# Order of the sign DMAs and the loads of q and k, and the engine of X's low part for two pairs of heads

## The chip, the core and the metric

The kernel runs on one core of a Trainium2 chip. The metric is the device time of one execution in microseconds, the median of several executions. A core has TensorE (PE, the matmuls; PEld its weight loads), VectorE (DVE), ScalarE (ACT), GpSimd (POOL) and SyncE (SP), which here only issues DMAs. Each engine works through its own instructions in order and waits for others at semaphores. SP's DMAs run on the core's 16 DMA engines.

## What is computed

Attention with a mask of hashed buckets, followed by a mixture of experts with a fixed capacity.

```python
def attn(q, k, v, proj):                      # q, k, v: 4 x 8 x 768 x 64, proj: 64 x 6
    q_bits = (q @ proj > 0); k_bits = (k @ proj > 0)
    q_bucket = sum(q_bits * 2**arange(6)); k_bucket = sum(k_bits * 2**arange(6))
    scores = where(q_bucket == k_bucket, q @ k.T / 8, -1e9)
    scores -= scores.max(-1)
    a = exp(scores); a /= a.sum(-1) + 1e-9
    return a @ v
def moe(x, w_gate, w1, w2):                   # x: 3072 x 512, 8 experts of 384 tokens each
    # tokens are taken in falling order of their best gate logits, until an expert is full
    out[tokens of e] = relu(x[tokens of e] @ w1[e]) @ w2[e]
```

## The kernel before

The 32 heads are worked in 8 groups G of 4 (head h is j = h % 4 of group h // 4); the operands of two groups are held at a time, in buffers u = G % 2. float32 accuracy is made of pairs of 16-bit values, a high and a low part: `QA`, `KA` hold the high parts of q and k of a head with further rows below them, `QB`, `KB` the high part of one and the low part of the other. Rows 64 to 69 of `QA` and `KA` hold the six signs of the projections (in tile `bt` until they are moved), as large plus and minus values, so that one matmul gives scores that are far lower wherever a bucket differs. Rows 96 to 99 of `QA` take the row maxima.

Time goes in steps t, six per head (192 in all, and a few behind), each of two half-steps n = 2t and 2t + 1. Within a step each engine's program is written out by hand in the order `ORD` (line 23): `S` passes of a head some 9 to 12 steps ahead (`S_pass`, line 259: two matmuls into `pss`, line 267, and the row maximum by DVE, line 269), then the score matmuls of the step's head in two halves (`ST`, line 306: lines 316 and 317 into `pst`, one of three buffers, and the exponential by ACT, line 318), the low part of the exponentials (`lo`, lines 322 and 325, by POOL or DVE), the matmuls with v four steps later (`AV`, lines 339 to 341), and whatever lists of half-steps (`P1` to `P4`, `Z3`, `Z4`, `MV`, `MD`) put at n.

These lists prepare the next group. For group G + 1 q and k are loaded (`load`, line 75; `qp` and `kp` have one buffer each; the issuing line is 77), ACT casts q and k to their high parts `qh` and `kh` in four pieces each (`cast`, line 148; q's from half-step 48G + 22 on, k's from 48G + 29 on, 48 half-steps being one group), negates them into `ql` and `kl` (`turn`, line 152; from 48G + 28 on), POOL's DMA adds the float32 values to these (`adds`, line 154), PE projects and DVE takes the signs (lines 168 and 172). At the end `sumv` (line 231) sums v with twelve matmuls.

`moves` (line 193) then brings group G's parts into `QA`, `KA`, `QB` and `KB` by DMAs of SP, in up to four portions. For G = 3 to 6 the order is the string `MO` (line 47): `A`, `B`, `K`, `L` are the high parts, `c` clears the maxima's rows (line 216), `s` is eight DMAs of signs (line 206), two per head, `q` and `k` are the loads of the next group, `l` and `m` the low parts (`kb<-kl`, `qb<-ql`). The bars part the portions; the third and fourth stand at half-steps 105 and 111 for G = 3 and at 48(G-1) + 8 and + 15 for G > 3. Between them lie, on SP, the DMAs of the maxima (`m_lay`, line 287, `qa<-mr`), behind them the transposes and stores of the attention's result (`xout`, lines 377 and 378). `turn` writes the tile `ql` that the DMA `m` of the group before has read.

For each pair of heads, `xlow` (line 367) subtracts the high part of the normalised result X (`XS`, cast by ACT, line 365) from X. It is emitted 4 half-steps behind the cast, for odd heads h = 1 to 29, on POOL where `XE[0] <= h <= XE[1]`, else on DVE.

`S_pass` and `ST` call `holds`, which counts what `wrote` noted of a buffer when the program is built; it makes no instruction.

Of the kernel before, what the change touches and what calls it, by code (L numbers as in the profile page):

```python
# [24 lines left out]
 E0=[3, 5],  # L25
 E1=[],
 X=[5, 4, 20, 15],
 XE=[9,25],
 MR=3,
 MT=4,  # L30
 LEAD=[9,12,40,4],
# [12 lines left out]
 Z4=[-20,-12,-18,-9,-12,-6],  # L44
 EA=[262, 32, 5],
 EG={2: 0, 3: 3},
 MO=['', 'AKs', 'BqL', 'lmk', 'c|ABqKLslmk', 'AB|KL|cs|qklm', 'AB|KL|cs|qklm'],
 MD=[[0, 2], [0, 5, 9, 15], [0, 2, 7, 14]],
 MV=[23, 24, 28, 57, 96, 1],
 WS=-23,  # L50
# [6 lines left out]
def attention(tc, nc, ctx, qT, kT, vv, proj, wg, x_dram, L, jp, identf, ident, B, late=None, after=None):  # L57
# [10 lines left out]
    def wrote(w,G): KEEP[w,G%2]=KEEP.get((w,G%2),[])+[G]  # L68
    def holds(G,**need):
        for w,n in need.items():  # L70
            if KEEP.get((w,G%2),[])[-n:]!=[G]*n: raise ValueError(f'{w} of group {G} is read out of turn')
# [3 lines left out]
    def load(G,w):  # L75
        if w==0: alloc_load(G)
        SY.dma_start(LD[G][w],(qT,kT,vv)[w][G])
# [13 lines left out]
    def warm(n,w=512):  # L91
        for _ in range(n): T.matmul(wps[:,0:w],wrm[:,0:128],wrm[:,0:w],start=True,stop=True)
# [17 lines left out]
    QA=[];KA=[];QB=[];KB=[];VH=[];VL=[];WF=[]  # L110
# [32 lines left out]
    def cast(G,w,p,half=None):  # L143
        if (G,'h') not in TMP:
            TMP[G,'h']=[dp.tile([128,2,S],F16,name=n,bufs=1) for n in ("qh","kh")]
            TMP[G,'l']=[dp.tile([128,2,S],F16,name=n,bufs=1) for n in ("ql","kl")]
        if half is None: A.copy(TMP[G,'h'][w][:,p],LD[G][w][:,p])
        else: A.copy(TMP[G,'h'][w][:,p,half*384:half*384+384],LD[G][w][:,p,half*384:half*384+384])
    def sub(G,w,p,eng=None):
        (eng or G_).tensor_tensor(TMP[G,'l'][w][:,p],LD[G][w][:,p],TMP[G,'h'][w][:,p],op=ALU.subtract)  # L150
# [18 lines left out]
    def signs(G):  # L169
        bt=TMP[G,'b']=dp.tile([128,S],F16,name="bt",bufs=1); b2=bt.rearrange("p (z q) -> p z q",z=2); z=0  # L170
        for ps in TMP[G,'p']:
            n=ps.shape[1]; V.tensor_scalar(b2[:,z:z+n],ps[:,:,0:384],0.0,0.5,op0=ALU.is_gt,op1=ALU.subtract); z+=n
        if G in (2,3): scaled(G)
        elif G<2: V.tensor_scalar(bt,bt,8192.0,None,op0=ALU.mult)
# [4 lines left out]
    def his(G):  # L179
        u=G%2; h=TMP[G,'h']  # L180
        for qk,(a,b,r0) in enumerate(((QA,QB,0),(KA,KB,64))):
            for r,j in sides(G): SY.dma_start(a[u][0:64,j,0:S],h[qk][r,1])
            wrote('hi',G)
            for r,j in sides(G): SY.dma_start(b[u][r0:r0+64,j,:],h[qk][r,1])
    def dbits(G):
        u=G%2; bt=TMP[G,'b']
        for hh in range(2):
            for w,dst in enumerate((QA,KA)): SY.dma_start(dst[u][64:70,2+hh,0:S],bt[64+32*w+6*hh:70+32*w+6*hh,:])
        wrote('sign',G)
    def lows(G):  # L190
        u=G%2; l=TMP[G,'l']
        for r,j in sides(G): SY.dma_start(KB[u][0:64,j,:],l[1][r,1]); SY.dma_start(QB[u][64:128,j,:],l[0][r,1])
        wrote('low',G)
    def moves(G,part=0):


        u=G%2; h=TMP[G,'h']; l=TMP[G,'l']; bt=TMP[G,'b']
        hs=[(slice(64*hh,64*hh+64),slice(hh,4,2)) for hh in range(2)]
        def go(dst,src,r0=0):
            for r,js in hs: SY.dma_start(dst[u][r0:r0+64,js,0:S],src[r])  # L200
            wrote('hi' if dst is QA or dst is KA else 'low',G)
        def signs_():
            for j in range(4):
                for w,dst in enumerate((QA,KA)):
                    a=64*(j//2)+32*w+6*(j%2)
                    SY.dma_start(dst[u][64:70,j,0:S],bt[a:a+6,:])
            wrote('sign',G)
        def nxt(w):
            if G+1<NG: load(G+1,w)
        todo=dict(A=(go,QA,h[0]),B=(go,QB,h[0]),K=(go,KA,h[1]),L=(go,KB,h[1],64),s=(signs_,),c=(clear,G),q=(nxt,0),k=(nxt,1),l=(go,KB,l[1]),m=(go,QB,l[0],64))  # L210
        for x in AP['MO'][part] if G==1 else AP['MO'][min(G+2,6)].split('|')[part]:
            f,*x=todo[x]; f(*x)
    def clear(G):
# [3 lines left out]
    def cv(G,j):  # L217
        A.copy(VH[G%2][:,j,:,0:64],LD[G][2][:,j]); wrote(f'vh{j}',G)
    def sv(G,j,e=None,n=1):
        for i in range(j,j+n): holds(G,**{f'vh{i}':1}); wrote(f'vl{i}',G)  # L220
        (e or V).tensor_tensor(VL[G%2][:,j:j+n],LD[G][2][:,j:j+n],VH[G%2][:,j:j+n,:,0:64],op=ALU.subtract)
# [36 lines left out]
    M6={}; passes={}; maxed=[]  # L258
    def S_pass(h,qc):
        G,j=divmod(h,4); u=G%2  # L260
        if G: holds(G,hi=2,sign=1)
        if G>1: holds(G,clear=1)
        passes[h]=passes.get(h,0)+1
        if qc==0: M6[h]=m8[h%3]
        ps=psS.tile([128,2,512],F32,name="pss")
        for hf in range(2):
            T.matmul(ps[:,hf,0:HK],QA[u][:,j,qc*128:qc*128+128],KA[u][:,j,hf*HK:hf*HK+HK],start=True,stop=True)  # L267
            if h==0: warm(DW[1],DW[4])
        V.tensor_reduce(M6[h][:,qc:qc+1],ps[:,:,0:HK],axis=AX.XY,op=ALU.max,negate=True)  # L269
# [19 lines left out]
    def m_rows(h,hf):  # L289
        G,j=divmod(h,4)  # L290
        if passes[h]<(6 if h>=2 else 3*hf+3): raise ValueError('a maximum is not whole')
        maxed.extend([(h,0),(h,1)] if h>=2 else [(h,hf)])
        if h>=2:
            ps=psS.tile([128,2,512],F32,name="pss")
            for c in range(6):
                T.matmul(ps[:,c//3,c%3*128:c%3*128+128],M6[h][:,c:c+1].to_broadcast([128,128]),ident,start=True,stop=True)
            A.activation(QA[G%2][96:128,j,:].rearrange("p (z q) -> p z q",z=2),ps[96:128,:,0:384],AF.Relu,bias=mbi[96:128],scale=msc[96:128])
            return
        MR[hf]=psT.tile([128,512],F32,name="pst")
        for c in range(3):  # L300
            T.matmul(MR[hf][:,c*128:c*128+128],M6[h][:,3*hf+c:3*hf+c+1].to_broadcast([128,128]),ident,start=True,stop=True)
        A.activation(QA[G%2][96:128,j,hf*384:hf*384+384],MR[hf][96:128,0:384],AF.Relu,bias=mbi[96:128],scale=msc[96:128])
# [3 lines left out]
    def ST(h,kc,hf):  # L306
        G,j=divmod(h,4); u=G%2
        if (h,hf) not in maxed or h>=8 and h not in laid: raise ValueError('a head has no maximum')
        if G: holds(G,hi=2,sign=1)
        if G: holds(G,low=4)  # L310
        if hf==0 and kc%2==0:
            pl=PT[h,-1-kc]=(dp.tile([128,2,S],F32,name="pt",bufs=4),dp.tile([128,2,S],F16,name="lo",bufs=4))
            for i in range(2): PT[h,kc+i]=(pl[0][:,i],pl[1][:,i])
        ps=psT.tile([128,512],F32,name="pst")
        r=slice(hf*384,hf*384+384); kr=slice(kc*128,kc*128+128)
        T.matmul(ps[:,0:384],KA[u][:,j,kr],QA[u][:,j,r],start=True,stop=False)  # L316
        T.matmul(ps[:,0:384],KB[u][:,j,kr],QB[u][:,j,r],start=False,stop=True)  # L317
        A.activation(PT[h,kc][0][:,r],ps[:,0:384],AF.Exp,scale=0.125)  # L318
# [83 lines left out]
    def add(n,f,*a):  # L402
        if n>=2*(6*NH+LAG+6): raise ValueError('an operation has no step')
        at.setdefault(n,[]).append((f,a))
    def bdma():
        for w,a in enumerate((QA,KA)): SY.dma_start(a[0][64:70,1,0:S],TMP[0,'b'][32*w:32*w+6])
    def copies(a):
        for j in (0,2): SY.dma_start(a[1][64:128,j:j+2,0:S],a[0][64:128,2:4,0:S])
    OPS=dict(i=lambda j: init(j,A.copy),t=top,b=lambda n: tbits(),k=behind,P=lambda n: project(0,[1]),r=lambda n: rest(n//3,n%3),l=lambda n: rlo(n//2,n%2),
        c=lambda w: cast(0,w,1),u=lambda w: sub(0,w,1),s=lambda k: S_pass(k//6,k%6),B=lambda n: signs(0),D=lambda n: bdma(),  # L410
        m=lambda n: m_rows(n//2,n%2),d=lambda n: dbits(0),f=lambda n: lows(0),g=lambda n: his(0),v=lambda j: cv(0,j),x=lambda j: sv(0,j,G_),
        e=lambda k: ST(0,k,0),C=lambda n: copies((QA,KA)[n]),w=lambda n: warm(n,DW[4]))
    n=-1; early=[]
    for o in AP['OPS'].split():
# [30 lines left out]
    k=12; done={}; S_at={}  # L445
# [7 lines left out]
    for h in range(1,NH,2):  # L453
# [7 lines left out]
        else:  # L461
            add(n,xhigh,4*b+d); add(n+AP['X'][1],xlow,4*b+d,G_ if AP['XE'][0]<=h<=AP['XE'][1] else V)
        if h==NH-1: pass
# [586 lines left out]
```

## Time and profile before

| | us |
|---|---|
| median of 3 runs | 703.2 (701.91 to 705.95) |
| the profiled execution | 703.8 |
| its span, first to last instruction | 701.9 |
| mean granted TensorE clock | 0.974 |
| PE busy | 654.6 (93%) |
| DVE busy | 515.6 (73%) |
| POOL busy | 518.3 (74%) |
| ACT busy | 393.3 (56%) |

The attention fills about the first 376 us, the experts the rest. A time in a row is counted from the first instruction. PE's matmuls are pipelined and their ends are modelled, so the start-to-start distance of two is shorter than the time of one. SP's instructions have a start and the time that SP was taken up by them; when their data landed is seen where another engine's wait for them ends. The granted clock is 1.00 at 2.4 GHz and 0.50 at 1.2 GHz.

### The profile page before, as it was taken

To read this page: it belongs to the slowest core of one execution; us is meant where nothing else is said; L and a number is where in the kernel's file an instruction comes from. 1 tells how busy PE (TensorE), PEld (TensorE's weight loads), DVE (VectorE), ACT (ScalarE), POOL (GpSimd) and SP (SyncE) were. 2 spreads that over 40 slices of the span, in tenths; PEclk is the share of its full clock that TensorE was granted. 3 is DMA by queue.
4 is the path that set the end of the run, shared out by engine and by line. 5 is a ranking of instruction groups with operands and counts; after the bars stand their busy time and mean duration, and the time that the engine had idled before them with its cause. 6 is when DMAs were issued, how large, how long until landed. Compare 5 with 4: busy or idle time off the path is not lost. (4 is left out here: it accounts for less than half of the span.)

```text
span 701.9 us, 19028 instructions
## 1 busy us (share of the span) xinstructions
PE 654.6 (93%) x7761; PEld 420.4 (60%) x7769; DVE 515.6 (73%) x1217; ACT 393.3 (56%) x805; POOL 518.3 (74%) x473
## 2 busy tenths in 40 slices
PE   8999999999898999999996699999999999999994
PEld 2566676767576776677675565545455555545551
DVE  7879798878777778698887849898979797913110
ACT  6877786777766777675571253526171716253620
POOL 7799987979689597988740553859787878787751
PEclk9999999999999999999997599999999999999998
DMA  8639579767898589862121534353534434363501
GB/s 222 178 112 233 152 186 171 177 124 146 213 164 166 123 150 226 135 147 47 26 57 36 159 129 165 136 195 136 193 138 169 161 139 178 120 225 135 196 31 45
DMA packets 64299, 102.54 MB, mean 146 GB/s; under 512 B 28960, under 2 KB 53588, under 8 KB 62164
## 3 DMA queue, kind: packets, MB, share of 16 engines
q1 hardware_dynamic: 55880, 51.24, 31.3%
q0 software_dynamic: 8224, 50.08, 23.9%
q8 instruction: 61, 1.00, 0.6%
q14 instruction: 26, 0.21, 0.1%
q10 hardware_dynamic: 108, 0.01, 0.0%
HBM read 67.39 MB, written 12.58 MB: 114 GB/s over the span
## 5 line engine op out<-in xcount | busy, mean ns | idle before, releaser
L322 POOL TENSOR_TENSOR lo<-pt 128x768 f16<-128x768 f32 x148 | 244.9, 1756 | 47.7 <-ACT pt L318 44.7
L318 ACT ACTIVATE pt<-pst 128x384 f32<-128x384 f32 x384 | 174.5, 493 | 77.0 <-PE pst L317 73.2
L269 DVE TENSOR_REDUCE m<-pss 128x1 f16<-128x770 f32 x192 | 181.4, 956 | 37.3 <-PE pss L267 36.5
L316 PE MATMUL pst<-qa,ka 128*128 128x384 f16 x384 | 124.7, 325 | 7.4 <-ACT pt L318 6.2
L341 PE MATMUL psv<-vh,lo 128*128 128x65 f16 x1152 | 124.4, 194 | 0.7 <-POOL lo L322 0.5
L317 PE MATMUL pst<-qb,kb 128*128 128x384 f16 x384 | 124.8, 325 | 0.0
L339 PE MATMUL psv<-vh,pt 128*128 128x65 f16 x1152 | 124.6, 195 | 0.2 <-DVE X L357 0.2
L340 PE MATMUL psv<-vl,pt 128*128 128x64 f16 x1152 | 124.6, 193 | 0.0
L339 PEld LDWEIGHTS <-pt 128*128 128x128 bf16 x1152 | 107.4, 98 | 15.4 <-issue 3.1
L340 PEld LDWEIGHTS <-pt 128*128 128x128 bf16 x1152 | 106.1, 99 | 11.2
L867 ACT CAST wh<-wf 128x1024 f16<-128x1024 f32 x64 | 65.4, 1042 | 79.0 <-DMA wf<-in_w_dram,zwidx 50.0
L341 PEld LDWEIGHTS <-lo 128*128 128x128 f16 x1152 | 106.2, 98 | 1.1 <-POOL lo L322 0.8
L267 PE MATMUL pss<-ka,qa 128*128 128x385 f16 x384 | 94.2, 328 | 5.1 <-DVE m L269 4.3
L879 POOL TENSOR_TENSOR wl<-wf,wh 128x512 bf16<-128x512 f32 x74 | 84.2, 1153 | 0.0
L902 PEld LDWEIGHTS <-wh 128*128 128x128 f16 x544 | 50.6, 99 | 30.6 <-issue 0.9
L858 POOL DMA_INDIRECT wf<-in_w_dram,zwidx x20 | 20.5, 1024 | 57.2 <-DVE zmi L791 30.6
L914 PEld LDWEIGHTS <-hh 128*128 128x128 f16 x384 | 35.5, 98 | 36.2
L902 PE MATMUL ph<-xx,wh 128*128 128x384 f16 (+1 forms) x304 | 56.9, 312 | 0.1
L317 PEld LDWEIGHTS <-kb 128*128 128x128 f16 x384 | 37.2, 97 | 31.8 <-issue 10.7
L316 PEld LDWEIGHTS <-ka 128*128 128x128 f16 x384 | 37.6, 98 | 25.2 <-issue 2.6
L902 PE MATMUL po<-xx,wh 128*128 128x384 f16 x240 | 48.1, 326 | 0.0
L989 POOL TENSOR_TENSOR wl<-wf,wh 128x512 bf16<-128x512 f32 x36 | 42.7, 1212 | 5.5 <-ACT wh L867 5.3
(293 smaller groups left out, 1222.1 us busy)
## 6 DMA issues: line engine op xcount, KB each, us to landing
vp<-in_vv_dram SPq DMA_DIRECT2D x8, 768.0 KB
x_dram<-XS SPq DMA_DIRECT2D x16, 384.0 KB
qp<-in_qT_dram SPq DMA_DIRECT2D x7, 768.0 KB
kp<-in_kT_dram SPq DMA_DIRECT2D x7, 768.0 KB
qa<-qh SPq DMA_DIRECT2D x14, 192.0 KB
ka<-kh SPq DMA_DIRECT2D x14, 192.0 KB
qb<-qh SPq DMA_DIRECT2D x14, 192.0 KB
kb<-kh SPq DMA_DIRECT2D x14, 192.0 KB
```

Of the source, the lines that this page charges most:

```text
L267: T.matmul(ps[:,hf,0:HK],QA[u][:,j,qc*128:qc*128+128],KA[u][:,j,hf*HK:hf*HK+HK],start=True,stop=True)
L269: V.tensor_reduce(M6[h][:,qc:qc+1],ps[:,:,0:HK],axis=AX.XY,op=ALU.max,negate=True)
L316: T.matmul(ps[:,0:384],KA[u][:,j,kr],QA[u][:,j,r],start=True,stop=False)
L317: T.matmul(ps[:,0:384],KB[u][:,j,kr],QB[u][:,j,r],start=False,stop=True)
L318: A.activation(PT[h,kc][0][:,r],ps[:,0:384],AF.Exp,scale=0.125)
L322: eng.tensor_tensor(l,p,p.bitcast(BF)[:,1::2],op=ALU.subtract)
L339: T.matmul(av[:,c,:],ph[:,r],VH[u][:,j,kc,:],start=(kc==0 and c==0),stop=False,skip_group_check=True)
L340: T.matmul(av[:,c,0:64],ph[:,r],VL[u][:,j,kc,:],start=False,stop=False,skip_group_check=True)
L341: T.matmul(av[:,c,:],l[:,r],VH[u][:,j,kc,:],start=False,stop=False,skip_group_check=True)
L867: s.nc.scalar.copy(h[:,r],f[:,r])
L879: for _ in range(n): s.nc.gpsimd.tensor_tensor(*s.pend.pop(0)[1],op=ALU.subtract)
L902: T.matmul(p[:,r],a[:,o:o+128],b[:,d,r],start=n==0 and not c,stop=n==11 and c in (None,2),skip_group_check=c is not None)
```

## The change

Three edits. In `MO`, for the groups 3 and above, the third portion was clear, all signs, and the fourth the loads of q and k and the low parts; now the third is clear, the signs of heads j = 0 and 1 (`e`), and the load of q, and the fourth is the load of k, the signs of heads j = 2 and 3 (`o`), and the low parts. `signs_` takes the heads as arguments, and `holds` asks for two notes of signs for j > 1. `XE` ends at 21 in place of 25, so `xlow` of the pairs that end in heads 23 and 25 is DVE's.

```diff
- XE=[9,25],
+ XE=[9,21],
...
- MO=['', 'AKs', 'BqL', 'lmk', 'c|ABqKLslmk', 'AB|KL|cs|qklm', 'AB|KL|cs|qklm'],
+ MO=['', 'AKs', 'BqL', 'lmk', 'c|ABqKLslmk', 'AB|KL|ceq|kolm', 'AB|KL|ceq|kolm'],
...
-        def signs_():
-            for j in range(4):
+        def signs_(*js):
+            for j in js:
                 for w,dst in enumerate((QA,KA)):
                     a=64*(j//2)+32*w+6*(j%2)
                     SY.dma_start(dst[u][64:70,j,0:S],bt[a:a+6,:])
             wrote('sign',G)
...
-        todo=dict(...,s=(signs_,),c=(clear,G),q=(nxt,0),k=(nxt,1),...)
+        todo=dict(...,s=(signs_,0,1,2,3),e=(signs_,0,1),o=(signs_,2,3),c=(clear,G),q=(nxt,0),k=(nxt,1),...)
...
-        if G: holds(G,hi=2,sign=1)
+        if G: holds(G,hi=2,sign=1+(G>2 and j>1))
```

## Rows read from the trace of the kernel before

**Rows 1.** Busy table of the page: busy us, share, instructions.
```profile
PE 654.6 (93%) x7761; PEld 420.4 (60%) x7769; DVE 515.6 (73%) x1217; ACT 393.3 (56%) x805; POOL 518.3 (74%) x473
```
**Rows 2.** PE's waits, 115 to 290 us: who <- for whom: us, times, longest.
```profile
PE pst L316 <- ACT pt L318: 6.0, 14, 1.1
PE pst L282 <- ACT pt L318: 1.2, 4, 0.3
```
**Rows 3.** ACT's waits, 115 to 290 us.
```profile
ACT qh L148 <- DMA qp<-in_qT_dram: 7.0, 4, 2.4
...
ACT ql L152 <- DMA qb<-ql: 3.2, 3, 1.1
```
**Rows 4.** Timeline of ACT: start, us, engine, line, operation, [idle before <- releaser].
```profile
177.45 0.51 ACT L148 CAST qh<-qp 128x384 f16<-128x384 f32 x1 [2.21 <-DMA qp<-in_qT_dram]
...
184.64 0.84 ACT L152 ACTIVATE ql<-qh 128x768 f16<-128x768 f16 x1 [1.00 <-DMA qb<-ql]
...
222.46 0.51 ACT L148 CAST qh<-qp 128x384 f16<-128x384 f32 x1 [2.38 <-DMA qp<-in_qT_dram]
```
**Rows 5.** Timeline of SP in the moves of group 4, from the fifth sign on.
```profile
168.29 0.66 SPq L206 DMA_DIRECT2D qa<-bt  x1
169.93 0.66 SPq L206 DMA_DIRECT2D ka<-bt  x1
...
172.43 0.68 SPq L287 DMA_DIRECT2D qa<-mr  x1
173.15 0.44 SPq L77 DMA_DIRECT2D qp<-in_qT_dram  x1
173.65 0.42 SPq L77 DMA_DIRECT2D kp<-in_kT_dram  x1
...
175.63 1.43 SPq L200 DMA_DIRECT2D qb<-ql  x2
```
**Rows 6.** Stretches: PE, PEld, DVE, ACT, POOL busy, granted clock, DMA share, GB/s.
```profile
172.00:174.00 2.00, 2.00 (x29) 1.42 (x27) 1.93 (x6) 1.76 (x5) 2.00 (x3) 1.00 0.11 25
176.00:178.00 2.00, 1.44 (x24) 0.94 (x23) 2.00 (x4) 0.55 (x2) 2.00 (x3) 1.00 1.07 332
182.00:184.00 2.00, 2.00 (x40) 1.54 (x36) 1.46 (x2) 1.26 (x3) 1.76 (x3) 1.00 1.41 154
```
**Rows 7.** Timeline of SP, moves of group 5: fifth sign and load of q.
```profile
212.43 0.66 SPq L206 DMA_DIRECT2D qa<-bt  x1
...
216.14 0.55 SPq L77 DMA_DIRECT2D qp<-in_qT_dram  x1
```
**Rows 8.** Timeline of ACT: the maxima that the DMA at 172.43 moves.
```profile
168.80 0.44 ACT L284 ACTIVATE mr<-pst,mb,ms 24x128 f16<-24x128 f32 x1
```
**Rows 9.** A stretch as in rows 6; line 231's matmuls (ns min/median/max, first and last start).
```profile
226.00:228.00 2.00, 2.00 (x13) 1.40 (x12) 0.00 (x0) 0.01 (x1) 2.00 (x2) 0.50 0.93 46
...
L231 PE MATMUL pst<-vl,on x6: 270/270/271, 180.5 to 181.6; 128*128 128x256 f16 x6
...
L231 PE MATMUL pst<-vl,on x6: 416/417/418, 225.5 to 227.6; 128*128 128x256 f16 x6
```
**Rows 10.** Timeline of POOL: X's low part of head 23; low parts around 331.
```profile
305.40 1.65 POOL L367 TENSOR_TENSOR XS<-X,XS 128x768 f16<-128x768 f32 x1
...
331.04 5.03 POOL L322 TENSOR_TENSOR lo<-pt 128x768 f16<-128x768 f32 x3 [0.48 <-ACT pt L318]
```
**Rows 11.** Timeline of DVE: a maximum near head 23's step; two subtractions of one size.
```profile
304.76 0.96 DVE L269 TENSOR_REDUCE m<-pss 128x1 f16<-128x770 f32 x1 [0.62 <-PE pss L267]
...
331.51 1.80 DVE L322 TENSOR_TENSOR lo<-pt 128x768 f16<-128x768 f32 x1
...
341.72 0.95 DVE L322 TENSOR_TENSOR lo<-pt 128x768 f16<-128x768 f32 x1
```
**Rows 12.** PE's waits, 296 to 345 us.
```profile
PE pss L267 <- DVE m L269: 0.8, 2, 0.4
PE pss L396 <- DVE m L269: 0.2, 1, 0.2
```

More of the change, by code (lines that the diff above doesn't have):

```diff
@@ L209, in nxt @@
             if G+1<NG: load(G+1,w)
-        todo=dict(A=(go,QA,h[0]),B=(go,QB,h[0]),K=(go,KA,h[1]),L=(go,KB,h[1],64),s=(signs_,),c=(clear,G),q=(nxt,0),k=(nxt,1),l=(go,KB,l[1]),m=(go,QB,l[0],64))
+        todo=dict(A=(go,QA,h[0]),B=(go,QB,h[0]),K=(go,KA,h[1]),L=(go,KB,h[1],64),s=(signs_,0,1,2,3),e=(signs_,0,1),o=(signs_,2,3),c=(clear,G),q=(nxt,0),k=(nxt,1),l=(go,KB,l[1]),m=(go,QB,l[0],64))
         for x in AP['MO'][part] if G==1 else AP['MO'][min(G+2,6)].split('|')[part]:
@@ L308, in ST @@
         if (h,hf) not in maxed or h>=8 and h not in laid: raise ValueError('a head has no maximum')
-        if G: holds(G,hi=2,sign=1)
+        if G: holds(G,hi=2,sign=1+(G>2 and j>1))
         if G: holds(G,low=4)
```

## The prediction

> **What bounds the kernel now.** I read the busy table first [rows 1]: TensorE is busy for 654.6 of 701.9 us, so the kernel gets faster only where TensorE stands still or runs slowly. In the steady part of the attention, 115 to 290 us, the waits of TensorE are nearly all for the exponentials of ScalarE [rows 2]: 6.0 us before the score matmuls and 1.2 us before the matmuls that turn the maxima. So the next view is what ScalarE itself waits for [rows 3]. Waits for TensorE are harmless there; two others are not: 7.0 us in four waits for the load of q, and 3.2 us in three waits for the DMA `qb<-ql`. ScalarE works in order, so the exponentials queued behind a waiting cast wait too, the score tiles fill up, and TensorE stops. The timeline shows both kinds [rows 4]: 2.21 us at 177.45 for q of group 5, 2.38 us at 222.46 for q of group 6, 1.00 us at 184.64 for `ql`. The four q waits belong to the loads of groups 4 to 7, one in each.
>
> Why q is late stands in the timeline of the DMA-issuing engine, SyncE [rows 5]: in group 4 the eight sign DMAs go out one after the other, about 0.70 us each; the maxima's row `mr` follows directly, at 172.43, and q only at 173.15. Meanwhile the DMA engines do next to nothing: 0.11 busy from 172 to 174, but 1.07 and 1.41 from 176 to 178 and 182 to 184 [rows 6]. The load stands behind small DMAs that are not urgent, with an idle stretch ahead of it.
>
> **The change part by part: order on SyncE, groups 3 to 6** (group 7 has no next load; its signs alone are split, which costs nothing, since the signs of heads 2 and 3 are read at least 24 half-steps later). It removes and adds no DMA. q moves ahead of four signs and of `mr`: it takes the place of the fifth sign, 168.29 instead of 173.15, 4.9 us earlier. In group 5's moves the same step is 212.43 against 216.14 [rows 7], 3.7 us earlier. Now q is in use 177.45 - 173.15 = 4.3 us after its issue in one, 222.46 - 216.14 = 6.3 us in the other. Taking those: in use at 172.6, wanted at 177.45 - 2.21 = 175.24; and at 218.7, wanted at 220.08. The smallest margin is 1.3 us, so the four q waits should go.
>
> Next is what else the queue does. `mr` is ready by 169.24 [rows 8], so it need not wait long. k follows `mr`. The sixth sign went out 0.98 us late although its tile was free; that looks like a limit on DMAs under way (the eighth DMA before it is the first `kb<-kh`), and I let `mr` and k meet that wait instead: `mr` about 169.9, k about 170.95 (now 173.65). Then the four late signs, 4 x 0.70 = 2.8 us, to about 174.2, then `kb<-kl` and `qb<-ql` at 174.2 and 175.7, where they are now (175.63 for the second pair). So the low parts are issued no earlier, but q (768 KB) and k have mostly passed by then.
>
> That matters: **the wait for `ql` decides whether the gain is kept.** If ScalarE loses its q wait it comes to the `ql` step 2.2 us earlier, at 183.64 - 2.21 = 181.4 in group 5; if `qb<-ql` still landed at 184.64 it would only wait there for 3.2 us. An estimate of when it lands after the change: the four low DMAs are 192 KB each; at the 200 GB/s or so between the 154 and 332 GB/s of [rows 6] that is 3.9 us; starting 1.4 us after the first issue (175.6), with 1 us to be seen, 180.5. That is 0.9 us before it is wanted.
>
> The sum, ScalarE waits against TensorE time. *q waits:* -7.0 us. Behind each, ScalarE has the exponentials that were held up to catch up on, and TensorE lives from these, so I take a wait that goes as time gained one for one; bounds 0 (given back at `ql`) and -7.0. *`ql` waits:* bounds 0 and -3.2; I take -2.0, because the casts of k and the sign turns that follow keep ScalarE fuller than TensorE and leave some of TensorE's wait in place. *Clock:* in the one group with the longest q wait the granted clock is 0.50 from 226 to 228, which is 1.2 GHz, after TensorE stood still at the q wait; six sum matmuls `pst<-vl` then start over 2.1 us, against 1.1 us in the group before [rows 9]. Without the halt I expect no fall: -1.0 us, bounds 0 and -1.8. The granted clock fell after only one of the four halts, so an uncovered halt elsewhere may cost as much.
>
> **X's low part of heads 23 and 25.** Each goes from GpSimd (1.65 us [rows 10]) to VectorE; 2 x 1.65 = 3.3 us leave GpSimd, which gains nothing, because TensorE's waits in this stretch are for VectorE's maxima, 0.8 and 0.2 us, and for no low part of GpSimd [rows 12]. VectorE takes a 128x768 subtraction in 0.95 us, or 1.80 us while GpSimd works beside it [rows 10, 11]. Head 23's falls near 305, where VectorE has one gap of 0.62 us [rows 11]; if the maxima behind it (`pss`) come late, TensorE waits for them. Cost of each: 0.95 - 0.62 = 0.3 us of lateness at best, 1.80 - 0.62 = 1.2 us at worst, part of which the two `pss` buffers absorb. I take +0.4 for both; bounds -0.3 (a shorter GpSimd queue) and +2.4.
>
> The Trainium skill (SBUF — State Buffer, Who interferes with whom) has a rule against this part: a VectorE operation with two SBUF inputs and a GpSimd operation that reads SBUF take the shared port in turn, and the later one blocks for the whole of the other. The trace agrees on the direction (0.95 against 1.80 us) but shows 0.85 us of it, not a whole operation of GpSimd; what a whole one would give is rival 5, 697.8 us.
>
> Sum: -7.0 - 2.0 - 1.0 + 0.4 = -9.6. The profiled execution took 703.8 us (span 701.9 and 1.9 around it), 0.6 above the median of 703.2. 703.8 - 9.6 = **694.2 us**.
>
> **The rivals.** *1. The wait moves to `ql`.* q is in time, but the low parts still land when they do now, for instance because each DMA lands about 8 us after its issue whatever is ahead (`qb<-ql` issued by 177.06, used at 184.64). For it: they are issued no earlier. Against it: the queue ahead of them is then q and k, 1.5 MB that go earlier. Then the gain is lost in the three groups with a `ql` wait and kept in group 6 alone, 2.4 + 1.0 - 0.4 = 3.0: 700.8 us. *2. Half comes back elsewhere:* TensorE moves up to other limits, VectorE's maxima or GpSimd's low parts, as both are busy over 70% of the span. -4.8: 699.0 us. *3. It does not do what it says:* q still goes out late, because SyncE is held before it by a buffer or by DMAs under way. Against it: nothing holds the fifth sign, and q's buffer is free, since the signs that are being sent were made from it. 703.8 + 0.4 = 704.2 us. *4. Slower: the four late signs push the low parts back.* Place: SyncE between k and `kb<-kl`. If `mr` or k go out no earlier than now, the 2.8 us of signs come on top, `qb<-ql` is issued 2.8 us later in each group, and ScalarE waits that much longer for `ql` in the three groups where it waits already: 3 x 2.8 = +8.4, 712.2 us. It decides from the point where `qb<-ql` lands later than at 184.64 in that stretch: each us beyond that costs up to 3. *5. X's low part waits for a whole operation of GpSimd,* 1.65 us [rows 10], before its own 0.95: 2.6 - 0.62 = 2.0 us of lateness for each, 4.0 in place of 0.4: 697.8 us. Against it: the subtraction beside GpSimd's took 1.80, not 2.6 [rows 11].
>
> **How the numbers follow.** Forecast 0.58 (its own range 691.5 to 697.5: all of the waits, the clock at 1.8 and X's part at -0.3 give 703.8 - 12.0 - 0.3 = 691.5; two thirds of the q waits and no gain of clock give 703.8 - 4.7 - 2.0 + 0.4 = 697.5); rival 2, 0.11; rival 5, 0.04; rival 1, 0.12; rival 3, 0.09; rival 4, 0.06. A measurement of this kernel can tell about 0.5%, 3.5 us, from no change. Faster by more than that: the forecast, rivals 2 and 5 and a third of rival 1's spread, 0.77; same: the rest of rival 1 and rival 3, 0.17; slower: 0.06. The range must leave out no more than 2 in 10, so it goes from 691.5 to 701.0, which takes in rivals 1, 2 and 5.
>
> **What would show it.** In the changed profile: q issued directly behind the fourth sign; no wait of a q cast for its load in groups 4 to 7; `qb<-ql` used before 181.4 on the old time scale, and the `ql` waits near 0; no fall of the granted clock at about 225 us; TensorE's wait for the exponentials from 115 to 290 us down from 6.0 to about 2 us; the attention's end some 9 us earlier and everything behind it only shifted. I am wrong if the q waits go and the `ql` waits grow by as much, if TensorE begins to wait for `pss` or low parts in their place, or if the q waits stay.

## The result and the profile after

The changed kernel takes 693.8 us (median of 6 executions, 691.99 to 698.64); the kernel before took 702.75 us beside it. The ratio is 0.988, 95% interval 0.984 to 0.992. In a second comparison, beside the last experiments, it was 692.64 against 706.22 us, ratio 0.984 (0.980 to 0.988). The kernel before was 3.5 us slower there, so across the two comparisons ratios are compared, not times. The profiled execution took 694.53 us, its span is 692.6.

The waits of ScalarE from 115 to 290 us come first, as in [rows 3] (who <- for whom: us, times, longest). The line of the q casts is gone, and of 3.2 us for `ql` 0.7 are left.

```profile
ACT pt L318 <- PE pst L317: 36.6, 55, 2.9
...
ACT ql L152 <- DMA qb<-ql: 0.7, 1, 0.7
```

TensorE's waits in the same stretch answer to [rows 2]: 6.0 us for the exponentials before the score matmuls became 2.4. A small new one, for VectorE's copy of the maxima (line 277), has come up in the place of the 1.2 us at line 282. The sums of v (line 231) waited as well; in the kernel before it was

```profile
PE pst L231 <- ACT pt L318: 1.2, 4, 0.3
```

and in the changed kernel:

```profile
PE pst L316 <- ACT pt L318: 2.4, 5, 0.9
PE pst L282 <- DVE m L277: 0.7, 3, 0.2
PE pst L231 <- ACT pt L318: 0.2, 1, 0.2
```

The timeline of SyncE in the moves of group 4, to be read beside [rows 5]: q directly behind the fourth sign, then the maxima, k, four signs, the low parts.

```profile
166.64 0.66 SPq L206 DMA_DIRECT2D ka<-bt  x1
167.34 0.44 SPq L77 DMA_DIRECT2D qp<-in_qT_dram  x1
168.65 0.69 SPq L287 DMA_DIRECT2D qa<-mr  x1
170.02 0.33 SPq L77 DMA_DIRECT2D kp<-in_kT_dram  x1
170.57 0.69 SPq L206 DMA_DIRECT2D qa<-bt  x1
...
173.48 1.38 SPq L200 DMA_DIRECT2D kb<-kl  x2
174.96 1.37 SPq L200 DMA_DIRECT2D qb<-ql  x2
```

ScalarE's timeline at the two steps of [rows 4]: neither has an idle time in front of it now.

```profile
174.03 0.50 ACT L148 CAST qh<-qp 128x384 f16<-128x384 f32 x1
...
180.46 0.83 ACT L152 ACTIVATE ql<-qh 128x768 f16<-128x768 f16 x1
```

The DMA engines, by stretches as in [rows 6]: the stretch in front of the q cast that was idle (0.11) is in use.

```profile
168.00:170.00 2.00, 2.00 (x37) 1.47 (x34) 0.96 (x1) 1.95 (x6) 2.00 (x2) 1.00 0.88 211
...
172.00:174.00 2.00, 2.00 (x35) 1.48 (x34) 2.00 (x2) 1.54 (x5) 2.00 (x4) 1.00 0.82 330
```

Where the time went is best read from two stretches that are cut at the first exponential of a head: heads 8 to 23, in which the moves of groups 3 to 6 lie, and heads 24 to 30, in which X's part lies. The columns are those of [rows 6]. The kernel before:

```profile
113.02:292.65 179.63, 170.50 (x2627) 122.06 (x2626) 138.44 (x194) 129.67 (x303) 146.44 (x122) 0.99 0.82 162
292.65:362.17 69.52, 68.04 (x1135) 51.27 (x1133) 58.69 (x85) 43.56 (x101) 57.03 (x38) 1.00 0.37 80
```

and the changed kernel:

```profile
113.70:283.39 169.69, 166.36 (x2627) 120.62 (x2626) 138.60 (x194) 129.91 (x303) 146.38 (x122) 1.00 0.81 172
283.39:351.96 68.57, 67.67 (x1135) 51.08 (x1134) 59.63 (x87) 43.40 (x100) 53.44 (x36) 1.00 0.38 81
```

So heads 8 to 23 are 9.94 us shorter and heads 24 to 30 0.95 us. Of the 9.94 us, 5.8 come out of TensorE's idle time (179.63 - 170.50 = 9.13 became 169.69 - 166.36 = 3.33); 4.1 come out of the time that the profile counts as busy, the fall of the clock of [rows 9] among them. So the waits that a view lists need not be all that the halts cost. What lies ahead of head 8 is 0.68 us longer (113.70 against 113.02), what lies behind the start of head 31 is 0.9 us longer (692.6 - 351.96 against 701.9 - 362.17). Neither is touched by the change. The sum is -9.3 us of span.

### The profile page after: what moved, and what is told of

It reads as the page before. It is cut to its first block, busy times and chain, and to the rows that moved or that the text cites. A ratio compares the mean times of both kernels' runs of the same rounds, so it can differ in the third digit from the quotient of the medians.

```text
span 692.6 us, 19032 instructions
## 1 busy us (share of the span) xinstructions
PE 649.3 (94%) x7769; PEld 419.3 (61%) x7769; DVE 517.2 (75%) x1219; ACT 393.6 (57%) x805; POOL 514.7 (74%) x471
```

## The experiments

The theory under test: ScalarE's waits for q and for `ql` held up the exponentials, TensorE lost about as much, and the new order takes both away; X's part is small. The table puts the two waits (summed over heads 8 to 23) beside the length of heads 8 to 23 and of heads 24 to 30 in each profiled execution, and the ratio of the times with its interval.

| kernel | waits for q, `ql` | heads 8 to 23 | heads 24 to 30 | ratio to before |
|---|---|---|---|---|
| before | 7.0 + 3.2 | 179.63 | 69.52 | 1 |
| changed | 0 + 0.7 | 169.69 | 68.57 | 0.988 (0.984 to 0.992) |
| changed, again | 0 + 0 | 169.42 | 68.59 | 0.984 (0.980 to 0.988) |
| order alone | 0 + 0 | 169.25 | 69.51 | 0.986 (0.982 to 0.990) |
| X's part alone | 7.5 + 3.7 | 178.58 | 68.58 | 1.002 (0.999 to 1.004) |
| low parts late | 0 + 6.3 | 175.76 | 68.58 | 0.998 (0.995 to 1.001) |
| q ahead of all signs | 0 + 5.7 | 174.53 | 68.59 | 0.992 (0.988 to 0.996) |
| q behind the maxima | 0 + 1.3 | 170.34 | 68.58 | 0.984 (0.980 to 0.988) |
| X's part of head 25 alone | 0 + 0.5 | 169.61 | 68.07 | 0.984 (0.980 to 0.988) |
| four signs last | 0 + 0 | 169.79 | 68.59 | 0.985 (0.982 to 0.988) |
| low parts, then q | 14.1 + 0 | 186.44 | 68.58 | one execution each: 710.54 against 707.83 us |

The granted clock fell in heads 8 to 23 once in the kernel before, once with the low parts late, once with q ahead of all signs, three times with the low parts ahead of q, and in none of the others.

**The new order alone.** The changed kernel with one line undone:

```diff
- XE=[9,21],
+ XE=[9,25],
```

> The new order of the sign DMAs and loads alone; X's low part of heads 23 and 25 stays on GpSimd. My theory (nearly the whole gain is ScalarE's waits for q and ql): no q wait in groups 4 to 7, the ql waits at 0.7 us or less, and a time of 694 to 696 us, that is 7.5 to 9 us below the kernel before. In heads 24 to 31 the trace of the changed kernel is about 1.0 us shorter than that of before, and I put that down to X's low part, so this kernel should lack it. Rival (X's part carries a good share, since it also frees GpSimd in the tail): 698 us or more.

Measured: 692.51 us, ratio 0.986; neither wait is left. The two stretches:

```profile
112.76:282.01 169.25, 166.24 (x2627) 120.70 (x2626) 138.64 (x194) 130.03 (x303) 146.41 (x122) 1.00 0.80 172
282.01:351.52 69.51, 68.03 (x1135) 51.25 (x1133) 58.67 (x85) 43.55 (x101) 56.98 (x38) 1.00 0.36 80
```

The order alone has the whole gain that the times show. The time is even 1.5 us below the lower end of what I expected, though heads 24 to 30 take 69.51 us as before.

**X's part alone.** The kernel before with `XE=[9,21]`:

```diff
- XE=[9,25],
+ XE=[9,21],
```

> X's low part of heads 23 and 25 on VectorE alone, order of DMAs as before. My theory: 701 to 703 us, about 1 us below the kernel before: a new wait of some 0.5 us of TensorE for VectorE in head 25, and head 28 about 1.4 us shorter, since VectorE's subtraction there no longer runs beside one of GpSimd (0.95 in place of 1.80 us). The four q waits stay, 7 us in all. My prediction's own figure for this part was +0.4 us, so 703 to 704. Rival (this part carries the gain): under 698 us.

Measured: 703.95 us, ratio 1.002 (0.999 to 1.004), no difference that can be seen. That is a miss of what I expected here (701 to 703 us) and lies where the prediction's own figure put it (703 to 704). The trace does show a difference:

```profile
115.08:293.66 178.58, 169.02 (x2627) 120.99 (x2626) 138.52 (x194) 129.52 (x302) 146.38 (x122) 1.00 0.81 163
293.66:362.24 68.58, 67.67 (x1135) 51.07 (x1134) 59.64 (x87) 43.40 (x100) 53.45 (x36) 1.00 0.40 81
```

Heads 24 to 30 take 68.58 us, as in each kernel with this part. The 0.94 us do not appear in the whole times, where what is ahead of head 8 and behind head 30 differs by as much and more from one execution to the next (head 8 starts 2.06 us later in this one than in the kernel before). The q waits are there as before (7.5 us). There is one more thing in this trace: the granted clock is 1.00 throughout heads 8 to 23, and though it waits a little longer than the kernel before, this stretch is 1.05 us shorter. I put that down to the one fall of the clock in the kernel before [rows 9].

**Low parts late.** The changed kernel with a fifth portion, 4 half-steps behind the fourth:

```diff
- 'AB|KL|ceq|kolm', 'AB|KL|ceq|kolm'
+ 'AB|KL|ceq|ko|lm', 'AB|KL|ceq|ko|lm'
- [0, 5, 9, 15], [0, 2, 7, 14]
+ [0, 5, 9, 15, 19], [0, 2, 7, 14, 18]
```

> The changed kernel with the low parts (kb<-kl, qb<-ql) of groups 3 to 7 in a portion of their own, 4 half-steps later, so that the transposes and stores of X go out before them; q is as early as in the changed kernel. Theory that the landing of qb<-ql decides whether the gain is kept: no q waits, but ql waits of 3 to 5 us in each of groups 4 to 7, and a time of 703 to 710 us, the gain given back or more. Rival (q's wait alone is the cost, and ScalarE has slack behind it): 693 to 697 us.

Measured: 701.74 us, ratio 0.998. q is in time everywhere, and the gain is given back, at the place that rival 1 named, though the waits are shorter (0.95 to 2.24 us in a group) and the time lower than I expected. The trace keeps more than the times do: heads 8 to 23 are 3.9 us shorter than in the kernel before, where the changed kernel has 9.94. A fall of the clock behind the first of its waits (1.98 us) is part of the loss. ScalarE's waits and the stretch:

```profile
ACT ql L152 <- DMA qb<-ql: 6.3, 4, 2.2
```

```profile
114.75:290.51 175.76, 168.73 (x2627) 121.56 (x2626) 138.72 (x194) 130.04 (x303) 146.21 (x122) 0.99 0.77 166
```

The reason for the smaller waits is on SyncE and ScalarE, group 4 (first the issue, then the wait):

```profile
173.06 0.37 SPq L77 DMA_DIRECT2D kp<-in_kT_dram  x1
...
180.57 1.61 SPq L200 DMA_DIRECT2D qb<-ql  x2
```

```profile
185.60 0.84 ACT L152 ACTIVATE ql<-qh 128x768 f16<-128x768 f16 x1 [0.95 <-DMA qb<-ql]
```

`qb<-ql` is issued by 182.18 and in use at 185.60: 3.4 us. In the kernel before it was 177.06 and 184.64, 7.6 us [rows 4, 5]. No load stood close ahead of it here, two did there. So its landing is not a fixed time behind its issue.

**q ahead of all signs.** The signs whole again, and q ahead of them (`holds` asks for one note of signs, as before):

```diff
- 'AB|KL|ceq|kolm', 'AB|KL|ceq|kolm'
+ 'AB|KL|cqs|klm', 'AB|KL|cqs|klm'
```

> q's load directly behind the clearing of the maxima's rows, ahead of all eight signs, which are not split; k's load and the low parts in the last portion. Theory (only the place of q counts, the splitting of the signs is one way to get there): no q waits and 693 to 696 us, as the changed kernel. Rival (the split matters, because k and the low parts come earlier by it, or because q's 768 KB collide with the high parts that are still under way): ql waits of 1 us or more per group remain and the time is 697 us or more.

Measured: 697.26 us, ratio 0.992; my theory in this form fell. The rival was right in the time, and in its `ql` waits for three of the four groups (0.87, 1.82 and 3.00 us). q is earlier than in any other kernel, and its waits are gone, yet 5.7 us of `ql` waits are left, the longest with a fall of the clock behind it. The stretch, and SyncE and ScalarE in group 4:

```profile
114.01:288.54 174.53, 168.59 (x2627) 121.19 (x2626) 138.69 (x194) 130.05 (x302) 146.54 (x122) 0.99 0.84 167
```

```profile
174.47 0.44 SPq L77 DMA_DIRECT2D kp<-in_kT_dram  x1
175.02 1.34 SPq L200 DMA_DIRECT2D kb<-kl  x2
176.46 1.26 SPq L200 DMA_DIRECT2D qb<-ql  x2
```

```profile
183.39 0.84 ACT L152 ACTIVATE ql<-qh 128x768 f16<-128x768 f16 x1 [1.82 <-DMA qb<-ql]
```

k's load went out right ahead of the low parts, because eight signs and the maxima were ahead of it. From the end of the issue (177.72) to the use it is 5.7 us: with both loads close ahead 7.6, with one 5.7, with none 3.4. Wherever ScalarE waited for `ql`, the span was 7.5 to 8.1 us with both (kernel before, X's part alone), 5.1 to 6.8 with one (this kernel) and 2.6 to 4.3 with none (low parts late, and the one wait left in each of three other kernels); an estimate from these is some 2 us for each load of 768 KB. The semaphore events in the traces, sixteen for each DMA, tell the landing itself. In group 4 k landed at 181.05 in the kernel before and at 179.80 here, and the low parts 3.5 us behind it both times; in the changed kernel k had landed at 175.72, before the second half of `qb<-ql` went out. That is what splitting the signs is for: it lets k out early too. That four signs then lie between k and the low parts is not what counts, as the run with these signs last shows below.

**q behind the maxima.** q one portion later:

```diff
- 'AB|KL|ceq|kolm', 'AB|KL|ceq|kolm'
+ 'AB|KL|ce|qkolm', 'AB|KL|ce|qkolm'
```

> The changed kernel with the load of q one portion later, behind the DMA of the maxima and directly ahead of the load of k; four of the signs are still behind both loads. Theory (q must be issued some 2 us earlier than before at least, and the low parts must have both loads behind them when they go out): q issued 1.5 to 3 us earlier than in the kernel before, q waits of 0 to 1 us each, ql waits between those of the changed kernel (0.7 us in all) and of the kernel before (3.2), 694 to 698 us. Rival (any order with four signs behind the loads is as good): 692 to 694 us.

Measured: 694.36 us, ratio 0.984, one `ql` wait of 1.3 us and no q wait. In group 4 q goes out 5.1 us ahead of its cast (171.93 and 177.07), where the kernel before left 2.1 us up to the moment when ScalarE wanted it (173.15 and 175.24) and the changed kernel leaves 6.7. On the times it can't be told from the changed kernel run beside it (692.64); the trace is 0.65 us longer in heads 8 to 23.

**Low parts, then q.** The opposite case: the low parts early, both loads behind them, q about where it was before:

```diff
- 'AB|KL|ceq|kolm', 'AB|KL|ceq|kolm'
+ 'AB|KL|ce|lmqko', 'AB|KL|ce|lmqko'
```

> The changed kernel with the low parts ahead of the two loads and four signs behind them: q is issued about when it was in the kernel before, but qb<-ql goes out earlier than anywhere so far. Theory (the two waits of ScalarE are one budget: a wait taken away at one place comes back at the other while a load or a low part still stands late in the queue): no ql wait, q waits of 2 to 4 us in each of groups 4 to 7, 8 to 14 us in all, and heads 8 to 23 take 177 to 182 us (169.7 in the changed kernel, 179.6 before), so 701 to 706 us. Rival (the low parts are the real limit, and q's place counts little): heads 8 to 23 under 174 us.

Measured in a single execution: 710.54 us, where the kernel before took 707.83; I had expected 701 to 706. The `ql` waits are gone and the q waits have doubled:

```profile
ACT qh L148 <- DMA qp<-in_qT_dram: 14.1, 4, 4.0
```

Heads 8 to 23 take 186.44 us, more than the 177 to 182 that I expected, in part since three of the four waits are followed by a fall of the granted clock. The whole stretch, and four microseconds behind the wait of 3.98 us at 182.96 (0.57 of full speed, that is most of the time at 1.2 GHz):

```profile
114.79:301.23 186.44, 172.58 (x2627) 123.46 (x2626) 138.63 (x194) 129.65 (x303) 146.58 (x122) 0.97 0.74 156
```

```profile
185.00:189.00 4.00, 3.77 (x30) 2.53 (x30) 0.00 (x0) 1.86 (x6) 3.79 (x6) 0.57 0.66 172
```

**Four signs last.** Ahead of them the low parts:

```diff
- 'AB|KL|ceq|kolm', 'AB|KL|ceq|kolm'
+ 'AB|KL|ceq|klmo', 'AB|KL|ceq|klmo'
```

> The changed kernel with the last four signs behind the low parts in place of ahead of them. Theory: qb<-ql goes out 2.8 us earlier, so no ql wait is left (0.7 us in the changed kernel, in group 7 alone), heads 8 to 23 take 169.0 to 169.4 us in place of 169.7, and the time is that of the changed kernel or up to 0.7 us less. Rival 4 of the prediction had the four signs push the low parts back: if they do so at a cost that the trace of the changed kernel hides, the time falls by over 2 us.

Measured: 695.3 us, ratio 0.985; no `ql` wait, but heads 8 to 23 take 169.79 us, not the 169.0 to 169.4 that I expected, and not less than in the changed kernel (169.69, run again 169.42). The four signs ahead of the low parts cost nothing in the changed kernel. Rival 4 is answered by this run.

**X's part of head 25 alone.** Head 23's back on GpSimd:

```diff
- XE=[9,21],
+ XE=[9,23],
```

> The changed kernel with X's low part of head 23 back on GpSimd; only head 25's is on VectorE. Theory (head 23's costs 0.5 us on VectorE, because it runs 2.2 us beside GpSimd; head 25's brings 1.4 us in head 28, where VectorE no longer runs beside GpSimd): heads 24 to 30 take 68.1 us, against 68.58 in the changed kernel and 69.51 with both on GpSimd. Rival (the two belong together, since GpSimd must be free for both): 69 us or more. On the whole time, 0.5 us below the changed kernel, which the times alone can hardly show.

Measured: 694.01 us, ratio 0.984. Heads 24 to 30 take 68.07 us, as expected:

```profile
284.75:352.82 68.07, 67.56 (x1135) 51.09 (x1134) 58.30 (x86) 43.43 (x101) 55.69 (x37) 1.00 0.40 82
```

So 1.45 us come from head 25's part and 0.5 us are lost to head 23's. On the whole time this is not to be seen.

**The changed kernel again**, with the last four:

> The changed kernel once more, to be compared on one chip with the next three and with the new order alone (692.5 us). Theory (X's part shortens heads 24 to 30 by 0.94 us and nothing else): 692 to 694 us. Rival (X's part costs something behind the attention that the traces of heads 24 to 30 do not show): 694 us or more.

Measured: 692.64 us (691.8 to 698.96), where the kernel before took 706.22. The new order alone (692.51) was measured beside a kernel before of 702.75, so the two times can't be compared as they stand; the ratios, 0.984 and 0.986, have intervals that overlap. No cost behind the attention is shown, and no gain of X's part either. None of these kernels is faster than the changed one by more than its executions scatter.

## Why the prediction was right, and where not

Predicted were 694.2 us; it is 693.8. That the two lie 0.4 us apart is luck: six executions of the changed kernel spread over 6.7 us, the sum starts from one profiled execution of 703.8 us where the kernel before has a median of 702.75, and the traces put the parts at -10.9 us (heads 8 to 23 and 24 to 30), not -9.6. The mechanism is not luck. Step by step:

**The q waits, -7.0.** Right. q went out directly behind the fourth sign, at 167.34 (I had worked out 168.29; group 3's waits, gone too, make this stretch earlier), all four waits are gone, and the waits, those for `ql` included, are worth most of their length in time: between the kernel with X's part alone and the changed one the clock is the same (1.00) and 10.5 us less of waits (11.2 to 0.7) give 8.9 us; between the kernel before and the changed one 9.5 us of waits and one fall of the clock give 9.94.

**The `ql` waits, -2.0.** The step was right, and it is the one that decides: the two kernels with q in time but the low parts behind something keep 5.7 and 6.3 us of `ql` waits and 5 to 6 us of the time. Of ScalarE's 3.2 us, 2.5 went in the first profile and all in the second. What that is worth in time can't be parted from the q waits: the two terms together were -9.0 us, and the two kernels without a fall of the clock give -8.9. Both of the kernels that keep `ql` waits also have one fall of the clock, which is part of their 5 to 6 us. I had feared that ScalarE is fuller than TensorE behind it; a remnant of that is TensorE's wait of 2.4 us for the exponentials.

**When the low parts land.** I had 180.5 for group 4; by the semaphore events they landed at 179.80, and `ql` found them in place at 180.46. (The 1 us for the landing to be seen, a term of that estimate, stands in no row.) That their time is set by what is ahead of them in the queue, not by a fixed 8 us, was an argument in the prediction; the three spans of 7.6, 5.7 and 3.4 us show it. Rival 1 was wrong for that reason.

**The clock, -1.0.** Borne out in this pair of profiles: an estimate of 1.05 us by the kernel with X's part alone, which has waits of about the same length (11.2 against 10.2 us) and no fall. That it always falls at such a wait, nobody should read from it: ScalarE stood still nearly as long in that kernel (2.26 us at most, against 2.38) and TensorE kept 2.4 GHz.

**X's low part, +0.4, bounds -0.3 to +2.4.** Wrong in sign and outside the bounds in the trace of heads 24 to 30: -0.94 us. I looked for the price at the step itself and missed what GpSimd's freed time does to VectorE later. At the step, head 23's part is dearer than my upper end of 1.80 us. Ahead of head 28, VectorE's subtraction of the same size as [rows 11]'s at 331.51 is back at 0.95, and an operation just before it (line 618) too is shorter, 0.30 us where it was

```profile
329.76 0.96 DVE L618 TENSOR_TENSOR zeq<-Lm,zm 128x144 f32<-128x144 f32 x1
...
331.04 1.47 POOL L322 TENSOR_TENSOR lo<-pt 128x768 f16<-128x768 f32 x1 [0.48 <-ACT pt L318]
```

in the kernel before (the second line is the first of the three operations of [rows 10]). Timelines of VectorE and GpSimd, changed kernel:

```profile
294.71 1.46 POOL L322 TENSOR_TENSOR lo<-pt 128x768 f16<-128x768 f32 x1
294.79 2.20 DVE L367 TENSOR_TENSOR XS<-X,XS 128x768 f16<-128x768 f32 x1
...
320.95 0.30 DVE L618 TENSOR_TENSOR zeq<-Lm,zm 128x144 f32<-128x144 f32 x1
322.03 0.95 DVE L322 TENSOR_TENSOR lo<-pt 128x768 f16<-128x768 f32 x1
322.29 2.02 POOL L322 TENSOR_TENSOR lo<-pt 128x768 f16<-128x768 f32 x1 [1.38 <-ACT pt L318]
```

TensorE's waits behind it, 290 to 345 us, in the changed kernel

```profile
PE psv L339 <- DVE X L357: 0.3, 1, 0.3
PE pss L267 <- DVE m L269: 0.3, 1, 0.3
```

and with the new order alone, where they are like [rows 12]:

```profile
PE pss L267 <- DVE m L269: 1.1, 3, 0.4
PE pss L396 <- DVE m L269: 0.2, 1, 0.2
```

One wait of TensorE for `X` came up (head 25, which is 0.5 us longer), most of those for the maxima went (head 28, which is 1.45 us shorter). GpSimd, without X's part, was done with its earlier operations when VectorE came to line 618, so VectorE began its subtraction 0.26 us ahead of GpSimd's next one; in the kernel before it began 0.47 us behind it ([rows 10, 11], 331.04 and 331.51).

The order of the two starts is what decides, and here I misread my own rows. VectorE's operation of 2.20 us ends 0.8 us behind the end of the GpSimd operation that began ahead of it (296.99 and 296.17), and so does its operation of 1.80 us in the kernel before (333.31 and 332.51). Where VectorE began first it took 0.95 us, and GpSimd's operation took 2.02 in place of 1.46. So the one that began later seems to have waited until the other was done. The Trainium skill (SBUF — State Buffer, Who interferes with whom) has it that a VectorE operation with two SBUF inputs contends with a GpSimd operation that reads SBUF, and that the shared ports are an exclusive lock; the trace agrees, with these ends. In the prediction I held against it that only 0.85 us were added, "not a whole operation"; but 0.47 us of GpSimd's operation were over by then. Rival 5 had the right mechanism with too high a price: head 23's part met nearly a whole operation, head 25's, which took 1.01 us, only the last 0.2 us of one. That the port is the reason is the page's account; the runs show the starts, the ends and whom they stand beside.

On the whole times the part stays open: X's part alone is 1.2 us above the kernel before, with an interval of -0.6 to +3.1 us (0.9992 to 1.0044 of 702.75), which holds my +0.4 and just leaves out the trace's -0.94.

**What was not tried.** The maxima's DMA went out 0.87 us after q's was issued (168.65 - 167.78), and k's 0.68 us after that; no run changed these gaps alone. What they are, the trace of the changed kernel shows: SyncE's own waits from 160 to 176 us name the landing of `kb<-kh`, the DMAs eight places ahead.

```profile
SPq L287 <- DMA kb<-kh: 0.8, 1, 0.8
SPq L77 <- DMA kb<-kh: 0.7, 1, 0.7
```

SyncE's DMAs signal their landing on eight semaphores in turn, so the "limit on DMAs under way" that the prediction suspected is, in this trace, a wait for the semaphore's last user; a limit of the chip is not shown.

## What to carry to other kernels

A load that is late behind small DMAs that can wait is found in three views: what the busy engine waits for, what that one waits for, and whether the DMA engines idle just before. When it is moved ahead, follow the next consumer of the same queue: here the low parts, further down, decided whether all, half or next to nothing of the 9 us was kept, and a load of 768 KB cost about 2 us (an estimate) to the transfers close behind it. A single execution's fall of the clock is worth about 1 us here and comes and goes, so stretches with and without one are not to be compared as if alike. Moving work between two engines that slow each other down has its effect also where they next run side by side, and there it is the order of the starts that has to be read.

## What the runs showed of the hardware

- TensorE's clock fell to 1.2 GHz behind some waits of ScalarE and not behind others of about the same length: behind one q wait of four in the kernel before (2.38 us, and not behind 2.21), three of four with the low parts ahead of q (2.89, 3.67 and 3.98 us, and not behind 3.57), none of four with X's part alone (2.26 us at most); behind a `ql` wait of 1.98 us and not behind one of 2.24 with the low parts late, and behind the one of 3.00 us with q ahead of all signs.
- VectorE's 128x768 subtraction took 0.95 us where it began ahead of GpSimd's, and up to 2.20 us where it began behind one, ending 0.8 us after it; GpSimd's, begun behind VectorE's, took 2.02 us in place of 1.46.
- The low parts landed 2.3 to 3.5 us behind the end of their issue in the changed kernel, where the loads were mostly over, and 6.7 to 8.0 us in the kernel before, with q's and k's loads of 768 KB each ahead of them.
- The first exponential came between 16.6 and 21.3 us in profiled executions of kernels that are the same up to there, head 8 between 112.8 and 116.7; what lies behind the start of head 31 took 338.3 to 340.7 us. In this scatter a gain of 1 us of the attention is lost from sight.
